# Block 3's x turned by DMA, its second half of attention earlier, and one pair's loads behind an x

## The chip, the cores and the metric

The kernel runs on one core of one Trainium2 chip. The metric is device time in microseconds: the median of several executions. The core has five engines that work side by side, each with its own instruction stream that it runs in order: TensorE (PE in the profile; its weight loads are PEld), VectorE (DVE), ScalarE (ACT), GpSimd (POOL) and SyncE (SP). In this kernel SP issues every DMA. An engine waits for another through semaphores, and everything behind a waiting instruction on its engine waits too.

## The reference, cut to what matters

Sliding-window attention over 8 batches, 8 heads, 576 positions and 64 dimensions, followed by a feed-forward layer with a squared relu:

```
scores = q @ k.T / 8                      # per batch and head
keep only 0 <= i - j < 64                 # causal window of 64 keys
attn   = softmax(scores) @ v
x      = attn, heads side by side         # 4608 tokens x 512
h      = relu(x @ w_in)                   # 512 x 2048
out    = (h * h) @ w_out                  # 2048 x 512
```

Inputs and output are float32; the kernel computes with float16 operands.

## The kernel before, in words

The 4608 tokens are 36 tiles of 128. Two neighbouring tiles are a pair, four tiles (512 tokens) are a block; there are nine blocks, 0 to 8. Pairs 10 and 15 (the names TAILS) hold the last 64 rows of the sequences and have loads of another shape.

For each pair, SP loads k, q and v into staging buffers (L121), POOL casts them to float16 (L269, for tails L761 and L771), and SP turns k and q with DMA transposes into kT and qT (L397). DVE copies the keys that reach over from the pair before (`halo_apart`, L335 to L339). For each tile, TensorE makes the scores (`S_`, L425), ACT the exponentials (`expo`, L431), DVE sets the masked ones to zero (`keep`, L436), TensorE multiplies by v (`V`, L448), and DVE divides by the sums into x_sb (`norm`, L456 and L457). Then x has to be turned, since the next product contracts over its 512 columns. There are two ways in the code: `X` with `copy_xT` turns a tile with four TensorE transposes (L468) into PSUM, and DVE copies it out (L269); `dma_xT` turns a whole pair with one DMA transpose from SP (L477). Either writes into xT, a tile for a block.

Per block, TensorE then makes the first feed-forward product (`UP`, 16 steps of four matmuls, L526). ACT makes the relu of each (L530), and the square is made by ACT (L533) or DVE (L536). The second product (`out_seven`, 14 steps of eight matmuls, L614) is a scheme of seven half-size products in place of eight; DVE makes the sums of operands that it needs (L602) at the start of a block and in between, and sums up and scales the results (L636), which SP stores (L651).

The order is written out by hand. A long list of words (FIRST) gives the order of the start. After it a loop over g from 2 to 9 collects events with due times between 0 and 1, sorts them and records them: the second product of block g − 1, the first product of block g, the attention of block g + 1, and the loads of pairs 2g + 3 and 2g + 4 with the next ones. So every engine's stream, and SP's queue too, follows the due times. `attention(g)` gives the due times of the two halves of a block (a half is a pair): scores at t + 0.02, the product with v at t + 0.25, turning x at t + dx. For block 3 alone, x is turned on TensorE and the times are shifted by 0.1. `loads(p)` gives k and q of pair p + h their transposes at t + 0.06, and asks for the loads of pair a + 1 at t + 0.14 (k and q; for a tail only k) and t + 0.3 (the rest), where a = p + h and t = 0.46 h. For a = 16 the first of them is at t + 0.28.

Buffers that matter here: scores, products with v and transposed x share two PSUM buffers of two banks (`att_bank`, the pool ps_att), taken in turn. The first product's results have two buffers of one bank each (ps_up).

In the profile, block 2's first product begins at 76 us, block 3's at 107 and block 4's at 136. Tiles 12 to 15 are block 3's, so their attention runs beside block 2's products.

Of the kernel before, what the change touches and what calls it, by code (L numbers as in the profile page):

```python
# [40 lines left out]
def kernel(  # L41
# [16 lines left out]
    TAILS = (10, 15)  # L58
# [27 lines left out]
    def later(n, fn):  # L86
        if n == 0:
            fn()
        else:
            put_off.append([n, fn])  # L90

    def tick():
        for e in list(put_off):
            e[0] -= 1
            if e[0] <= 0:
                put_off.remove(e)
                e[1]()
# [65 lines left out]
    def fetch_tail(nm, p):  # L163

        src = {"k": k, "q": q, "v": v}[nm]
        for i in (2 * p, 2 * p + 1):
            if nm == "q":
                if i % 2 == 0:
                    st = two_tiles()
                sts[nm, i] = st[:, i % 2]  # L170
                for n in range(2):
                    fetch_rows(sts[nm, i], src, tail_seq(i) + n, S - 64, 64, 64 * n)
            else:
                st = sts[nm, i] = two_tiles()
                for n in range(2):
                    fetch_rows(st[:, n], src, tail_seq(i) + n, S - 128)
# [88 lines left out]
    def copy(eng, out, in_, scale=1.0):  # L265
        if eng is nc.scalar:
            nc.scalar.activation(out=out, in_=in_, func=AF.Copy, scale=scale)  # L267
        elif scale == 1.0:
            eng.tensor_copy(out=out, in_=in_)  # L269
        else:  # L270
            eng.tensor_scalar(out=out, in0=in_, scalar1=scale, scalar2=None, op0=ALU.mult)
# [19 lines left out]
    def cast_q(i, eng=nc.gpsimd):  # L291
        copy(eng, pair16(q16s, "q16", i // 2)[:, i % 2], sts["q", i])

    def cast_v(i, eng=nc.gpsimd):
        copy(eng, v_evs[i % NV][:, :, 0:D], sts["v", i])
# [15 lines left out]
    def xT_of(g):  # L311
        if g not in xTs:
            xTs[g] = xtp.tile([P, 4, DMC, P], FP16, name="xT", tag="xT")
        return xTs[g]
# [37 lines left out]
    def att_bank(name, dtype=FP32):  # L352
        return ps_att.tile([P, 2, 512], FP32, name=name, tag="ps_a")
# [59 lines left out]
    def S_(i):  # L413
        sc = att_bank("sc")
        scv = sc[:].rearrange("p a (h b t) -> p a h b t", h=HP, b=2)
        for a in range(2 if i < 4 else 0):
            nc.tensor.matmul(sc[:, a, :], ident[:], minus[i > 0], start=True, stop=False,
                             skip_group_check=True)
        for hp in range(HP):
            for blk in range(2):  # L420
                for hh in range(2):
                    r0 = 64 * hh
                    qT = q_cols(i)[r0:r0 + 64, hp, :]
                    qT = qT[:, 64 * blk:64 * blk + 64]
                    nc.tensor.matmul(scv[:, hh, hp, blk, :], keys(i, hp, r0, blk), qT,  # L425
                                     start=i >= 4, stop=True, skip_group_check=i < 4)
        scs[i] = sc
        pms[i] = attw.tile([P, 2, HP * 2 * 64], FP16, name="pm", tag="pm")

    def expo(i, part=slice(0, 2)):  # L430
        nc.scalar.activation(out=pms[i][:, part], in_=scs[i][:, part], func=AF.Exp,  # L431
                             scale=1.0 / float(D) ** 0.5)

    def keep(i, part=slice(0, 2)):
        mask = mask_first if is_first(i) else mask_inner
        nc.vector.tensor_tensor(  # L436
            out=pms[i][:, part], in0=pms[i][:, part],
            in1=mask[:].rearrange("p (o a) r -> p o (a r)", o=1)
            .to_broadcast([P, part.stop - part.start, 512]), op=ALU.min)

    def V(i):
        ps = att_bank("av")
        avs[i] = ps[:, :, 0:4 * 66].rearrange("p a (h e) -> p a h e", h=4)
        for h in range(H):
            for blk in range(2):
                vv = (v_ods if blk == 0 else v_evs)[i % NV]
                h0 = h // 2 * P + blk * 64
                nc.tensor.matmul(  # L448
                    avs[i][64 * blk:64 * blk + 64, h // 4, h % 4, 0:65],
                    pms[i][:, h % 2, h0:h0 + 64], vv[:, h, 0:65], start=True, stop=True)  # L450

    def norm(i):
        if i // 2 not in xs:
            xs[i // 2] = attw.tile([P, 2, 2, HP, D], FP16, name="x_sb", tag="x_sb", bufs=2)
        rden = smallp.tile([P, 2, 4, 1], FP32, name="rden", tag="rden")
        nc.vector.reciprocal(out=rden[:], in_=avs[i][:, :, :, 64:65])  # L456
        nc.vector.tensor_tensor(  # L457
            out=xs[i // 2][:, i % 2], in0=avs[i][:, :, :, 0:D],
            in1=rden[:].to_broadcast([P, 2, 4, D]), op=ALU.mult)

    def xT_cols(i):
        return xT_of(i // 4)[:, i % 4]

    def X(i):
        xps[i] = att_bank("xt_ps")[:, 0, :].bitcast(FP16)[:, 0:DMC * P].rearrange(
            "p (c t) -> p c t", c=DMC)
        for c in range(DMC):
            nc.tensor.transpose(out=xps[i][:, c, :],  # L468
                                in_=xs[i // 2][:, i % 2, c // 2, 2 * (c % 2):2 * (c % 2) + 2, :],
                                identity=ident[:])  # L470

    def copy_xT(i, eng=nc.vector):
        copy(eng, xT_cols(i), xps[i])

    def dma_xT(p):

        nc.sync.dma_start_transpose(  # L477
            out=xT_of(p // 2)[:, p % 2 * 2:p % 2 * 2 + 2].rearrange("p n c t -> p (n c) t"),
            in_=xs[p][:].rearrange("p n a h d -> p (n a h d)"))
# [236 lines left out]
    def attention(g):  # L716
        c = 4 * g
        ev = []
        dx = 0.34 if g == 3 else 0.275

        def sc(i):
            S_(i)
            expo(i)
            later(2, lambda: keep(i))
            tick()

        def to_xT(i):
            if g == 3:
                X(i)
                copy_xT(i)  # L730
                tick()
            else:
                if i % 2:
                    dma_xT(i // 2)

        def va(i):
            V(i)
            norm(i)
            tick()

        for h in range(2):
            a, b, t = c + 2 * h, c + 2 * h + 1, 0.46 * h + (0.1 if g == 3 else 0.0)
            ev += [(t + 0.02, lambda a=a: sc(a)), (t + 0.021, lambda b=b: sc(b)),
                   (t + 0.25, lambda a=a: va(a)), (t + 0.251, lambda b=b: va(b)),
                   (t + dx, lambda a=a: to_xT(a)), (t + dx + 0.0001, lambda b=b: to_xT(b))]
        return ev

    def load(p, part):

        if p in TAILS:  # L750
            for nm in part:
                fetch_tail(nm, p)
        else:
            for nm in part:
                fetch_two(nm, p)
        both = (2 * p, 2 * p + 1)
        if "k" in part:
            for i in both:
                if p in TAILS:
                    k16s["tail", i] = st16.tile([P, 2, H, D], FP16, name="k16", tag="k16")  # L760
                    nc.gpsimd.tensor_copy(out=k16s["tail", i][:], in_=sts["k", i][:])  # L761
                else:
                    cast_k(i)
        if "q" in part:
            for i in both:
                cast_q(i)
        if "v" in part:
            for i in both:
                if p in TAILS:
                    for n, vv in enumerate((v_ods, v_evs)):  # L770
                        nc.gpsimd.tensor_copy(out=vv[i % NV][:, :, 0:D], in_=sts["v", i][:, n])  # L771
                else:
                    cast_v(i)
                    shift_v(i)

    def loads(p):

        ev = []
        for h in range(2):
            t, a = 0.46 * h, p + h  # L780
            if a < NCK // 2:
                ev.append((t + 0.06, lambda a=a: (dma_k(a), dma_q(a))))
                if a not in TAILS:
                    ev.append((t + 0.3, lambda a=a: halo_apart(a)))
            if a + 1 < NCK // 2:
                kq = "k" if a + 1 in TAILS else "kq"
                ev.append((t + (0.28 if a - 1 == TAILS[1] else 0.14), lambda a=a, x=kq: load(a + 1, x)))
                ev.append((t + 0.3, lambda a=a, x=kq: load(a + 1, "kqv"[len(x):])))
        return ev

# [3 lines left out]
    for g in range(2, NTB + 1):  # L794
# [3 lines left out]
        ev = even(out_seven(g - 1))  # L798
# [39 lines left out]
```

## Time and profile before

| | us |
|---|---|
| median of four runs (293.86 to 294.89) | 294.04 |
| profiled execution | 294.03 |
| its span, first to last instruction | 292.0 |
| PE busy | 283.6 (97%) |
| DVE busy | 212.4 (73%) |
| ACT busy | 192.2 (66%) |
| POOL busy | 114.4 (39%) |

A row of the timeline has the start in us from the span's start, the busy time of the row's instructions together, the engine, the line, the operation, what it writes and reads, the shapes and the number of instructions; a bracket tells the idle time before it and what ended it. SPq is SP's queue: the time shown is that of issuing, and the data land some microseconds later. The busy times of matmul rows overlap, since matmuls are pipelined.

### The profile page before, as it was taken

What the parts mean: (1) busy time and instruction counts of PE and PEld (TensorE: products, weight loads), DVE (VectorE), ACT (ScalarE), POOL (GpSimd) and SP (SyncE); (2) the same over time, 40 slices, a digit from 0 to 9 for tenths busy, and PEclk for the clock granted to TensorE, in tenths of its full rate; (3) what the DMA queues carried; (4) which work ended last, traced back from release to release, by engine and by line L of the source; (5) the groups of instructions that cost most, each with busy time, mean ns of one, the idle gap of its engine ahead of it and who ended that gap; (6) DMA issues with size and microseconds to landing.
All of it is one profiled execution on the core that took longest, in us unless ns stands there. A gap on an engine that the chain in (4) does not pass through costs nothing.

```text
span 292.0 us, 7468 instructions
## 1 busy us (share of the span) xinstructions
PE 283.6 (97%) x3039; PEld 195.8 (67%) x3039; DVE 212.4 (73%) x392; ACT 192.2 (66%) x304; POOL 114.4 (39%) x171
## 2 busy tenths in 40 slices
PE   4999999999999999999999999999999999999995
PEld 2678888755666666666666666666666666666684
DVE  3669999867958777776877688768776876555393
ACT  2789898968685666756675767576757675666500
POOL 3703986864348503314555735242455400000000
PEclk9999999999999999999999999999999999999999
DMA  8999999996799168899999999999979801300133
GB/s 217 321 394 318 290 294 323 332 257 147 214 236 238 37 207 192 200 174 263 221 251 196 233 226 187 158 206 231 237 169 259 194 2 50 132 0 2 72 108 110
DMA packets 151842, 57.64 MB, mean 197 GB/s; under 512 B 128256, under 2 KB 143616, under 8 KB 151808
## 3 DMA queue, kind: packets, MB, share of 16 engines
q1 hardware_dynamic: 151808, 57.16, 81.4%
q8 instruction: 24, 0.39, 0.5%
q14 instruction: 10, 0.08, 0.1%
HBM read 38.80 MB, written 9.44 MB: 165 GB/s over the span
## 4 chain that ended last, share of the span: by engine, by line
PE 88%; DVE 5%; DMA 3%; ACT 2%; POOL 0%; issue 0%; SPq 0%
PE hps L526 32%; PE opsC L614 10%; PE opsD L614 8%; PE hps L498 8%; PE opsA L614 8%; PE ops L574 5%; PE opsB L614 4%; PE av L448 4%; PE sc L425 3%; DMA k_st<-in_k_dram 1%; DMA xT<-x_sb 1%; DVE hs_all L602 1%; PE qT_ps L373 1%; DVE pm L436 1%; PE kT_ps L373 1%; PE warm L545 1%
## 5 line engine op out<-in xcount | busy, mean ns | idle before, releaser
L526 PE MATMUL hps<-xT,w_in_sb 128*128 128x512 f16 x448 | 112.9, 379 | 0.4 <-DVE h L536 0.2
L530 ACT ACTIVATE hrelu<-hps 128x512 f32<-128x512 f32 x112 | 66.7, 597 | 64.2 <-PE hps L526 63.9
L614 PEld LDWEIGHTS <-h 128*128 128x128 f16 x624 | 60.4, 98 | 20.7 <-issue 0.2
L526 PEld LDWEIGHTS <-w_in_sb 128*128 128x128 f16 x448 | 42.2, 98 | 33.4 <-DMA xT<-x_sb 0.4
L536 DVE SCALAR_TENSOR_TENSOR h<-hps,hrelu 128x512 f16<-128x512 f32 x54 | 37.2, 689 | 32.8 <-ACT hrelu L530 32.6
L269 POOL COPY v_od<-v_ev 64x512 f16<-64x512 f16 x54 | 37.3, 691 | 10.6 <-ACT v_ev L267 6.8
L431 ACT ACTIVATE pm<-sc 128x1024 f16<-128x1024 f32 (+1 forms) x40 | 35.3, 940 | 4.2 <-PE sc L425 4.2
L533 ACT ACTIVATE h<-hrelu 128x512 f16<-128x512 f32 x58 | 36.5, 629 | 1.6
L614 PE MATMUL opsA<-w_out_sb,h 128*128 128x256 f16 x240 | 31.0, 273 | 0.0
L614 PE MATMUL opsD<-wb_all,h 128*128 128x256 f16 x240 | 31.0, 273 | 0.0
L614 PEld LDWEIGHTS <-hs_all 128*128 128x128 f16 x256 | 25.0, 98 | 8.6
L498 PE MATMUL hps<-xT,w_in_sb 128*128 128x256 f16 x256 | 30.1, 273 | 0.0
L498 PEld LDWEIGHTS <-w_in_sb 128*128 128x128 f16 x256 | 24.2, 98 | 2.9
L457 DVE TENSOR_TENSOR x_sb<-av,rden 128x512 f16<-128x512 f32 x36 | 24.9, 691 | 1.2
L269 POOL CAST k<-kq_st 128x512 f16<-128x512 f32 x17 | 11.6, 686 | 33.8 <-DMA kq_st<-in_k_dram 33.7
L436 DVE TENSOR_TENSOR pm<-pm,mask_inner 128x1024 f16<-128x1024 f16 x25 | 20.1, 807 | 5.7 <-ACT pm L431 5.7
L269 POOL CAST q<-kq_st 128x512 f16<-128x512 f32 x22 | 14.7, 669 | 16.5 <-DMA kq_st<-in_q_dram 16.4
L636 DVE SCALAR_TENSOR_TENSOR osb_all<-opsD,u 128x512 f32<-128x512 f32 x14 | 9.7, 692 | 11.2 <-PE opsD L614 11.0
L614 PE MATMUL opsC<-w_out_sb,h 128*128 128x256 f16 x128 | 16.4, 273 | 0.0
L614 PE MATMUL opsB<-wb_all,hs_all 128*128 128x256 f16 x128 | 16.4, 273 | 0.0
L614 PE MATMUL opsC<-w_out_sb,hs_all 128*128 128x256 f16 x128 | 16.4, 273 | 0.0
L269 POOL CAST v_ev<-kq_st 128x512 f16<-128x512 f32 x16 | 11.6, 728 | 12.2 <-DMA kq_st<-in_v_dram 11.7
(103 smaller groups left out, 372.7 us busy)
## 6 DMA issues: line engine op xcount, KB each, us to landing
kq_st<-in_k_dram SPq DMA_DIRECT2D x26, 256.0 KB, 3.8
kq_st<-in_v_dram SPq DMA_DIRECT2D x24, 256.0 KB, 3.8
out_dram<-osb_all SPq DMA_DIRECT2D x12, 512.0 KB, 4.3
kq_st<-in_q_dram SPq DMA_DIRECT2D x18, 256.0 KB, 4.1
v_st<-in_v_dram SPq DMA_DIRECT2D x16, 256.0 KB, 5.3
k_st<-in_k_dram SPq DMA_DIRECT2D x7, 512.0 KB, 5.9
q_st<-in_q_dram SPq DMA_DIRECT2D x7, 512.0 KB, 5.8
out_dram<-osb_all SPq DMA_DIRECT2D x11, 256.0 KB, 2.4
```

Of the source, the lines that this page charges most:

```text
L269: eng.tensor_copy(out=out, in_=in_)
L431: nc.scalar.activation(out=pms[i][:, part], in_=scs[i][:, part], func=AF.Exp, scale=1.0 / float(D) ** 0.5)
L436: nc.vector.tensor_tensor(out=pms[i][:, part], in0=pms[i][:, part], in1=mask[:].rearrange("p (o a) r -> p o (a r)", o=1) .to_broadcast([P, ...
L448: nc.tensor.matmul(avs[i][64 * blk:64 * blk + 64, h // 4, h % 4, 0:65], pms[i][:, h % 2, h0:h0 + 64], vv[:, h, 0:65], start=True, stop=True)
L457: nc.vector.tensor_tensor(out=xs[i // 2][:, i % 2], in0=avs[i][:, :, :, 0:D], in1=rden[:].to_broadcast([P, 2, 4, D]), op=ALU.mult)
L498: nc.tensor.matmul(hps[:, f, :], w_in_sb[:, c, (2 * j + f) * P:(2 * j + f + 1) * P], xT_of(p // 2)[:, n0:n0 + 2, c, :], start=(c == 0), st ...
L526: nc.tensor.matmul(hps[:], w_in_sb[:, c, f * P:(f + 1) * P], xT_of(g)[:, :, c, :], start=(c == 0), stop=(c == DMC - 1))
L530: nc.scalar.activation(out=hrelu[:], in_=hps[:], func=AF.Relu)
L533: later(2 if f == 0 else 0, lambda: nc.scalar.activation(out=h2_of(g)[:, f, :], in_=hrelu[:], func=AF.Square))
L536: nc.vector.scalar_tensor_tensor(out=h2_of(g)[:, f, :], in0=hps[:], scalar=0.0, in1=hrelu[:], op0=ALU.max, op1=ALU.mult)
L574: nc.tensor.matmul(ops_of[ts][:], h2s[0][:, f, ts * P:(ts + 1) * P], w_out_sb[:, f, :], start=(f == 0), stop=(f == FFC - 1))
L614: nc.tensor.matmul(rows_of(bank, m), a[:, kk, m * P:(m + 1) * P], w[:, kk], start=(first and kk == 0 and (m == 0 or bank in apart)), stop= ...
```

## The change

For block 3, x is turned by `dma_xT` as in the blocks behind it, at t + 0.275. The half that starts at t = 0.56 starts at 0.38; the first stays at 0.1. In `loads`, k and q of pair 11 (a = 10, the first tail pair) are asked for at 0.46 + 0.28 = 0.74 instead of 0.60, which in SP's queue is behind the xT of pair 9, due at 0.735. For a = 16 nothing changes, since TAILS[1] + 1 is 16.

```diff
     def attention(g):
         c = 4 * g
         ev = []
-        dx = 0.34 if g == 3 else 0.275
...
         def to_xT(i):
-            if g == 3:
-                X(i)
-                copy_xT(i)
-                tick()
-            else:
-                if i % 2:
-                    dma_xT(i // 2)
+            if i % 2:
+                dma_xT(i // 2)
...
         for h in range(2):
-            a, b, t = c + 2 * h, c + 2 * h + 1, 0.46 * h + (0.1 if g == 3 else 0.0)
+            a, b = c + 2 * h, c + 2 * h + 1
+            t = (0.1, 0.38)[h] if g == 3 else 0.46 * h
             ev += [(t + 0.02, lambda a=a: sc(a)), (t + 0.021, lambda b=b: sc(b)),
                    (t + 0.25, lambda a=a: va(a)), (t + 0.251, lambda b=b: va(b)),
-                   (t + dx, lambda a=a: to_xT(a)), (t + dx + 0.0001, lambda b=b: to_xT(b))]
+                   (t + 0.275, lambda a=a: to_xT(a)), (t + 0.2751, lambda b=b: to_xT(b))]
...
                 kq = "k" if a + 1 in TAILS else "kq"
-                ev.append((t + (0.28 if a - 1 == TAILS[1] else 0.14), lambda a=a, x=kq: load(a + 1, x)))
+                ev.append((t + (0.28 if a in (TAILS[0], TAILS[1] + 1) else 0.14), lambda a=a, x=kq: load(a + 1, x)))
                 ev.append((t + 0.3, lambda a=a, x=kq: load(a + 1, "kqv"[len(x):])))
```

## The prediction

> **What bounds the kernel now.** I read the busy totals of the page first, then the engine sums over the two stretches that the change touches.
>
> ```profile
> PE 283.6 (97%) x3039; PEld 195.8 (67%) x3039; DVE 212.4 (73%) x392; ACT 192.2 (66%) x304; POOL 114.4 (39%) x171
> 85.00:106.00 21.00, 21.00 (x261) 14.21 (x260) 15.84 (x32) 12.47 (x21) 12.06 (x17) 1.00 0.65 154
> 106.00:136.00 30.00, 29.94 (x318) 19.79 (x312) 21.21 (x37) 20.30 (x33) 8.84 (x12) 1.00 1.00 204
> ```
>
> In the second and third line the columns are the stretch in us, its length, busy time of PE, weight loads, DVE, ACT and POOL, granted clock, DMA share and GB/s. TensorE has work in every microsecond of both (21.00 of 21.00, 29.94 of 30.00) at full clock. So only two things shorten the run: fewer TensorE instructions, or a gap between them that closes. The DMA engines have room in the first stretch (0.65) and none in the second (1.00). The timeline of TensorE then gives the price of each piece by the distance from one start to the next, since the ends are modelled and overlap.
>
> ```profile
> 85.66 1.04 PE L526 MATMUL hps<-xT,w_in_sb 128*128 128x512 f16 x4
> 86.54 1.04 PE L614 MATMUL opsB<-wb_all,hs_all 128*128 128x256 f16 x8
> 87.25 0.69 DVE L457 TENSOR_TENSOR x_sb<-av,rden 128x512 f16<-128x512 f32 x1
> 87.41 1.03 PE L526 MATMUL hps<-xT,w_in_sb 128*128 128x512 f16 x4
> 88.28 0.61 PE L468 MATMUL xt_ps<-ident,x_sb 128*128 128x128 f16 x8
> 88.72 1.04 PE L614 MATMUL opsC<-w_out_sb,hs_all 128*128 128x256 f16 x8
> ```
>
> A group of four L526 or eight L614 matmuls takes 0.87; the eight transposes of two tiles take 88.72 − 88.28 = 0.44.
>
> **Part 1, the transposes leave TensorE.** Tiles 12 to 15 lose X: two groups of eight (88.28, and 102.30 to 102.74), 2 × 0.44 = **−0.88**. All of it is on the path, since TensorE has no idle time there. The four copies xT on DVE (two rows of 0.74 for two) and nothing else go with them; DVE is busy 15.84 of 21.00 and doesn't set the end, so these count zero.
>
> In their place SP issues two DMA transposes, 1.24 us each in an unhurried queue. The row for xT says "DMA to landing us min/median/max: 2.7/3.9/4.7" over ten. The first waits for the second norm of pair 6, at 87.25 + 0.69 = 87.94. SP has issued the v of pair 8 by 84.6 and now stands 3.3 us. Behind it queue, in this order, the k and q of pair 8 (turned at 84.73 and 87.02 before, now about 89.2 and 90.7), four loads of pair 9 (were 88.31 to 91.4, now about 92 to 95), the second xT, two loads of pair 9's v, and the out stores (101.97, which wait for DVE anyway). What is late: k of pair 8 is first read by DVE's halo copy near 98; from 89.2 even the longest kT landing of the trace, 7.4, gives 96.6. Pair 9's v casts end on POOL near 105 instead of 100, and POOL waits from there to 113 for the next load. SP reaches the out stores near 99.5, ahead of their data. So this is hidden, and SP is back in step at 102.
>
> The second xT: V of tiles 14 and 15 now stands at 94.4 to 95.1, the norms take 1.7 us on DVE (86.19 to 87.94 in the pair before), so it is issued near 96.8 and lands near 100.7, 101.5 at the longest. Its reader, the first L526 of block 3, stood at 106.89 and comes to about 106.2. Cover of 4.7 us: zero.
>
> **Part 2, the second half's attention comes sooner.** S of tiles 14 and 15 moves from 92.29 to right behind opsB. This puts a new wait on TensorE. The attention banks are a pool of two: S14 takes the bank of av 12 and S15 that of av 13, which DVE frees at 87.94. TensorE reaches S14 at 87.41 + 0.10 (the gap that every S and V group has ahead of it, as 91.33 to 92.29 is 0.96) = 87.51, and S15 at 87.51 + 0.57/2 = 87.80. It can start 0.05 after DVE's end, 87.99: **+0.19**. Bounds: 0 if the groups lie a little later, 0.6 if DVE's norm is slowed. Behind S15 the whole of TensorE waits, nothing else.
> The two exponentials (1.92 for both) move to 88.0 to 89.9 on ACT. The relu behind them ends at 90.5; the bank it frees is wanted at 91.8. The DVE row of squares that frees the next bank comes to 92.7 against 93.5. Both covered by about 1 us.
>
> **Part 3, pair 11's k and q behind x of pair 9.**
>
> ```profile
> 126.05 1.26 SPq L397 DMA_TRANSPOSE qT<-q  x1
> 127.36 2.07 SPq L121 DMA_DIRECT2D kq_st<-in_k_dram  x2
> 129.48 2.32 SPq L121 DMA_DIRECT2D kq_st<-in_q_dram  x2
> 131.90 2.13 SPq L477 DMA_TRANSPOSE xT<-x_sb  x1
> 136.07 0.55 PEld L526 LDWEIGHTS <-w_in_sb 128*128 128x128 f16 x4 [0.42 <-DMA xT<-x_sb]
> ```
>
> The xT of pair 9 lands at 131.90 + 4.13 = 136.03 and the first L526 of block 4 starts at 136.08. The chain shows this DMA with 1.4% of the span, but the loss is only the gap: opsA in front starts at 134.89 and takes 0.87, so 136.08 − 135.76 = 0.32. Its data (norm of tile 19) are ready at 127.55 + 0.69 = 128.24. After the change it goes out then, shifted with TensorE to near 127.6, and lands by 132.3: **−0.32**, with 3 us to spare.
> What is late next: k and q of pair 11 go out 1.4 us later, and v at about its old time. POOL's casts of q move from 133.78 and 135.03 to about 135.3 and 136.8, v stays near 137.4. This is where DVE makes its sums for block 4 (L436 and L602, from 135.97, now 135.3). The trace has the same meeting two blocks on:
>
> ```profile
> 195.20 1.07 POOL L771 CAST v_od<-kq_st 128x512 f16<-128x512 f32 x1
> 195.82 0.98 DVE L602 TENSOR_TENSOR hs_all<-hs_all,h 128x1024 f16<-128x1024 f16 x1
> 197.74 1.09 DVE L602 TENSOR_TENSOR hs_all<-h 128x1024 f16<-128x1024 f16 x1
> 202.78 1.02 PE L526 MATMUL hps<-xT,w_in_sb 128*128 128x512 f16 x4 [0.17 <-DVE h L536]
> ```
>
> Alone these DVE rows take 0.69 and the cast 0.61. Block 6 has five longer ones, 1.79 us more in all, and TensorE loses 0.34 at 202.78. Block 5 has three (1.09 more) and loses nothing; block 4 now has two. So DVE's slack is about 1.45. The Trainium skill, page "SBUF — State Buffer", section "Who interferes with whom", speaks against the change here: a DVE operation with two SBUF inputs contends with a GpSimd operation that reads SBUF, and the later one blocks until the other has finished. Taken as it stands, up to 0.61 for each of six, 3.7 − 1.45 = 2.2 us of loss; by the rows, 0.40 for each of six at most, 2.4 − 1.45 = 0.95, and for four longer ones 1.6 − 1.45 = 0.15. POOL has a pause near 136 and its copies of 64 partitions slow DVE less than every time (140.05 took 0.69 beside one). I take **+0.10**; bounds 0 and 0.95.
>
> The k of pair 11 lands at 144.22 (7.1 after its issue at 137.09) and DVE's halo copy starts at 144.52. After the change SP gets there at 136.4 to 137.3: its queue runs 0.7 earlier and loses up to 0.9 waiting for the norm. It lands at 143.5 to 144.4, and DVE wants it near 143.5. DVE has 1.09 us of idle time before its next square (146.37), so a wait of up to 0.9 costs zero.
>
> **Sum.** −0.88 + 0.19 − 0.32 + 0.10 = −0.91. The profiled execution took 294.03 (span 292.0 and 2.0 around it), 0.01 from the median of 294.04: 293.12, so **293.1 us**, span 291.1. From block 5 on all queues hang on TensorE's and DVE's data and move along.
>
> **Rivals.**
> - Full gain (both new costs nothing): −1.20, 292.8. For it: the bank and DVE are each within 0.2 us of being ready. Against: 87.94 is DVE's end whatever TensorE does.
> - Most of it given back: DVE and POOL meet in all six rows (0.7 to 0.95) or S15 waits 0.6. Then −0.2 to −0.6, around 293.6. For it: block 6. Against: block 5.
> - No effect: an equal wait takes the place of the transposes, 294.0. It needs an xT that is late by 0.9 at 106.2, so landed at 107.1, 10.3 after issue; the longest is 4.7.
> - **Slower:** k of pair 11 is late. DVE stands in order at the halo copy, the squares behind it hold the hps banks, TensorE stops. It costs nothing until about 144.6, then one for one; to end 0.88 above the median the wait must give 1.8, so a landing after 146.4, 10 us after issue, against 7.4 for the longest of 13. With 146.7 the time is 295.2. For it: the DMA share from 136 to 150 is 1.19, and this landing was among the slowest. Against: the bytes ahead of it are the same.
>
> **Numbers.** 0.3% is 0.88 us, about what a measurement can tell from no change. My forecast 0.52 (own range 292.7 to 293.4; 0.40 of it below 293.16, 0.12 above), full gain 0.10, most given back 0.17, no effect 0.09, slower 0.12. Faster 0.50, same 0.38, slower 0.12. The range that leaves out the slower case and some per cent below is 292.7 to 294.1.
>
> **What would show it.** No L468 after 76 us; block 3's first opsA 0.6 to 0.8 earlier (105.3); a gap of 0.1 to 0.3 in the S matmuls near 87.8, ended by DVE L457; the L526 near 135 without a wait for xT; DVE's L602 of block 4 at 0.98 to 1.09 more often than two times; the halo copy near 143.5 with less than 1 us of idle time ahead. Wrong if S15 waits above 0.6, if an L526 of block 3 waits for xT, if DVE waits for kT near 98 or 143, or if a gap opens later than 150 that wasn't there.

## The result, and the profile after

The changed kernel takes 292.93 us (median of 39 runs, 291.77 to 295.03), against 294.14 for the kernel before on the same chip (60 runs). The ratio is 0.9959 with a 95% interval of 0.9948 to 0.9971: 1.2 us faster, between 0.85 and 1.53. The profiled execution took 292.79 with a span of 291.1 (before: 294.03 and 292.0).

First the page's busy totals of the changed kernel, and the engine sums over the two stretches that the prediction read.

```profile
PE 282.9 (97%) x3023; PEld 194.7 (67%) x3023; DVE 212.6 (73%) x388; ACT 192.6 (66%) x304; POOL 113.5 (39%) x171
85.00:106.00 21.00, 20.93 (x252) 13.95 (x248) 15.36 (x29) 13.47 (x21) 11.14 (x17) 1.00 0.86 185
106.00:136.00 30.00, 30.00 (x313) 19.72 (x311) 21.62 (x38) 20.30 (x32) 9.18 (x13) 1.00 1.07 212
```

PE has 16 matmuls fewer and DVE 4 rows fewer: the transposes and their copies. TensorE is still busy in all but 0.07 us of the 51, at a granted clock of 1.00, so it still sets the end. The DMA share of the first stretch rose from 0.65 to 0.86.

What TensorE loses at a place is worked out below by starts, as in the prediction: the distance from one start to the next, less what the same distance takes elsewhere. The idle time in a bracket is not the same number, since the ends of matmuls are modelled.

Next the timeline around the new place of the second half's scores, weight loads and DVE alone.

```profile
87.05 0.69 DVE L457 TENSOR_TENSOR x_sb<-av,rden 128x512 f16<-128x512 f32 x1
87.31 0.10 PEld L425 LDWEIGHTS <-kh 64*128 64x128 f16 x2 [0.21 <-issue]
87.79 0.29 PEld L425 LDWEIGHTS <-kT 64*128 64x128 f16 x16 [0.19 <-DVE x_sb L457]
88.13 0.55 PEld L526 LDWEIGHTS <-w_in_sb 128*128 128x128 f16 x4
```

The two score tiles take 0.82 from 87.31 to the next group; two tiles elsewhere take 0.57 (in the profile before, 92.29 to 92.86). The wait for DVE's L457, which frees the bank, has therefore cost 0.25.

The last of these views is SP's queue with TensorE at the start of stage 4.

```profile
127.44 1.35 SPq L477 DMA_TRANSPOSE xT<-x_sb  x1
128.84 1.20 SPq L121 DMA_DIRECT2D kq_st<-in_k_dram  x2
130.09 1.64 SPq L121 DMA_DIRECT2D kq_st<-in_q_dram  x2
134.06 1.05 PE L614 MATMUL opsA<-w_out_sb,h 128*128 128x256 f16 x8
134.83 0.64 PEld L526 LDWEIGHTS <-w_in_sb 128*128 128x128 f16 x4
134.94 1.03 PE L526 MATMUL hps<-xT,w_in_sb 128*128 128x512 f16 x4
```

The xT of pair 9 goes out ahead of pair 11's k and q, lands at 131.16 and is read at 134.94 without a wait; the 0.32 that stood here before is gone.

That is not the whole of it. The marks below are the starts of the first opsA row of each pass of the loop; the pass for g is called stage g, and a stage's time holds all its gaps. The prediction calls the start of stage 3 "block 3's first opsA". The expectations go by the block whose second product begins there: their "block 1's first opsA" is the start of stage 2.

| us, one profile each | start of stage 2 | stage 2 | stages 3–4 | stages 5–6 | stages 7–8 | stage 2 to last matmul | median (runs) | ratio, 95% |
|---|---|---|---|---|---|---|---|---|
| before | 75.35 | 30.66 | 58.12 | 58.09 | 54.25 | 213.51 | | |
| changed | 75.38 | 29.80 | 57.80 | 58.07 | 54.59 | 212.66 | 292.93 (39) | 0.9948–0.9971 |
| e1 x by DMA alone | 75.24 | 29.83 | 58.09 | 58.04 | 54.54 | 212.88 | 293.75 (22) | 0.9966–1.0002 |
| e2 load move alone | 74.40 | 30.93 | 57.81 | 57.81 | 54.84 | 213.77 | 294.15 (14) | 0.9976–1.0022 |
| e3 without load move | 74.60 | 29.86 | 57.92 | 57.81 | 54.58 | 212.56 | 293.84 (22) | 0.9976–1.0016 |
| e4 second half at 0.42 | 76.30 | 30.68 | 57.80 | 57.97 | 54.59 | 213.43 | 293.96 (14) | 0.9970–1.0008 |
| e5 second half at 0.46 | 75.77 | 29.61 | 58.11 | 57.89 | 54.25 | 212.24 | 293.13 (22) | 0.9930–0.9965 |
| e6 old times, both others | 74.71 | 29.55 | 57.81 | 57.98 | 54.59 | 212.31 | 292.94 (14) | 0.9938–0.9976 |
| e7 pair 11 still later | 76.25 | 29.92 | 58.48 | 57.93 | 54.59 | 213.30 | 293.84 (18) | 0.9965–1.0001 |
| e8 v loads later | 74.80 | 29.84 | 57.80 | 57.78 | 54.25 | 212.06 | 293.25 (19) | 0.9947–0.9985 |
| e9 0.46, v later | 76.25 | 29.76 | 57.83 | 58.17 | 54.25 | 212.40 | 292.59 (12) | 0.9915–0.9969 |
| e10 old times, v later | 75.61 | 29.74 | 57.80 | 57.90 | 54.25 | 212.08 | 292.58 (10) | 0.9920–0.9970 |
| e11 0.42, masks put off | 74.87 | 30.33 | 57.80 | 57.96 | 54.59 | 213.07 | 292.69 (1) | |
| e12 changed, again | 74.54 | 30.24 | 57.80 | 57.83 | 54.54 | 212.80 | 293.44 (12) | 0.9942–0.9988 |

The median of before beside e1 to e4 was 294.35, beside e5 to e8 294.55, beside e9 to e12 294.19; each ratio is the one on record against runs on the same chip, and is not the quotient of the two medians (for e3 that would be 0.9983). Three things are to be read from this table. The intervals of e1 to e4 and of e7 include 1: by time alone these five are not shown to be faster, and what is said of them below rests on one profile each. The start of stage 2 moves between 74.40 and 76.30, although the work up to there is the same in all of them, so single times carry noise larger than most effects in question; the columns behind it are free of that part. And stages 7–8, which the change doesn't touch, take 54.25 before and 54.59 after.

Where those 0.34 us went shows in the timeline of the changed kernel: DVE's sums with POOL's casts and copies at the start of stage 7, and the first product behind them.

```profile
222.48 0.82 POOL L269 CAST q<-kq_st 128x512 f16<-128x512 f32 x1 [0.34 <-DMA kq_st<-in_q_dram]
222.74 1.10 DVE L602 TENSOR_TENSOR hs_all<-h 128x1024 f16<-128x1024 f16 x1
223.45 0.86 POOL L269 CAST v_ev<-kq_st 128x512 f16<-128x512 f32 x1 [0.15 <-DMA kq_st<-in_v_dram]
223.87 0.98 DVE L602 TENSOR_TENSOR hs_all<-hs_all,h 128x1024 f16<-128x1024 f16 x1
224.38 1.96 POOL L269 COPY v_od<-v_ev 64x512 f16<-64x512 f16 x2
225.79 1.10 DVE L602 TENSOR_TENSOR hs_all<-h 128x1024 f16<-128x1024 f16 x1
226.40 0.95 POOL L269 CAST v_ev<-kq_st 128x512 f16<-128x512 f32 x1
226.92 0.98 DVE L602 TENSOR_TENSOR hs_all<-hs_all,h 128x1024 f16<-128x1024 f16 x1
230.83 0.59 PE L526 MATMUL hps<-xT,w_in_sb 128*128 128x512 f16 x2 [0.18 <-DVE h L536]
```

Five of DVE's six rows at the start of the stage (two masks, L436, and four sums, L602) take 0.98 to 1.10 in place of 0.69 (1.80 us more in all), the squares behind them are late, and TensorE waits for one. Each of the longer rows began while a POOL row ran, and ended 0.54 or 0.55 after that POOL row had ended: 222.48 + 0.82 = 223.30 against 222.74 + 1.10 = 223.84, then 224.31 against 224.85, 226.34 against 226.89, and 227.35 against 227.90. So DVE stood until POOL was done. Before, the six rows were 1.30 longer and nothing waited.

### The profile page after: what moved, and what is told of

It is laid out like the page before. It is cut to its first block, busy times and chain, and to the rows that moved or that the text cites. A ratio compares the mean times of both kernels' runs of the same rounds, so it can differ in the third digit from the quotient of the medians.

```text
span 291.1 us, 7442 instructions
## 1 busy us (share of the span) xinstructions
PE 282.9 (97%) x3023; PEld 194.7 (67%) x3023; DVE 212.6 (73%) x388; ACT 192.6 (66%) x304; POOL 113.5 (39%) x171
## 4 chain that ended last, share of the span: by engine, by line
PE 81%; DVE 8%; DMA 4%; SPq 3%; ACT 3%; issue 1%; ACTq 0%
PE hps L526 29%; PE opsC L614 10%; PE hps L498 9%; PE opsD L614 9%; PE opsA L614 6%; PE ops L574 5%; PE opsB L614 4%; DMA wb_all<-in_moe_w_in_dram 4%; PE av L448 3%; DVE hs_all L602 3%; PE sc L425 3%; DVE x_sb L457 2%; SPq L130 1%; SPq L121 1%; DVE pm L436 1%; ACT pm L431 1%
## 5 line engine op out<-in xcount | busy, mean ns | idle before, releaser
L526 PE MATMUL hps<-xT,w_in_sb 128*128 128x512 f16 x448 | 113.0, 379 | 0.3 <-DVE h L536 0.3
L526 PEld LDWEIGHTS <-w_in_sb 128*128 128x128 f16 x448 | 42.2, 98 | 32.9 <-issue 0.7
L536 DVE SCALAR_TENSOR_TENSOR h<-hps,hrelu 128x512 f16<-128x512 f32 x54 | 37.2, 689 | 32.2 <-ACT hrelu L530 32.0
L269 POOL COPY v_od<-v_ev 64x512 f16<-64x512 f16 x54 | 38.6, 715 | 8.2 <-ACT v_ev L267 4.3
L457 DVE TENSOR_TENSOR x_sb<-av,rden 128x512 f16<-128x512 f32 x36 | 24.9, 691 | 1.2
L436 DVE TENSOR_TENSOR pm<-pm,mask_inner 128x1024 f16<-128x1024 f16 x25 | 19.9, 803 | 3.9 <-ACT pm L431 3.9
L636 DVE SCALAR_TENSOR_TENSOR osb_all<-opsD,u 128x512 f32<-128x512 f32 x14 | 9.7, 692 | 11.6 <-PE opsD L614 11.6
```

The source lines that it names most:

```text
L436: nc.vector.tensor_tensor(out=pms[i][:, part], in0=pms[i][:, part], in1=mask[:].rearrange("p (o a) r -> p o (a r)", o=1) .to_broadcast([P, ...
L457: nc.vector.tensor_tensor(out=xs[i // 2][:, i % 2], in0=avs[i][:, :, :, 0:D], in1=rden[:].to_broadcast([P, 2, 4, D]), op=ALU.mult)
L526: nc.tensor.matmul(hps[:], w_in_sb[:, c, f * P:(f + 1) * P], xT_of(g)[:, :, c, :], start=(c == 0), stop=(c == DMC - 1))
L536: nc.vector.scalar_tensor_tensor(out=h2_of(g)[:, f, :], in0=hps[:], scalar=0.0, in1=hrelu[:], op0=ALU.max, op1=ALU.mult)
L636: nc.vector.scalar_tensor_tensor(out=dst, in0=banks[bank][:, ms], scalar=OUT_SCALE, in1=sums[add][:, ms], op0=ALU.mult, op1=ALU.add)
```

## The experiments

All of them compute the full output.

**Each part alone.** First, x by DMA with the due times and the load as before; second, the load move without the rest; third, the changed kernel without the load move.

```diff
 e1, against the kernel before
-        dx = 0.34 if g == 3 else 0.275
+        dx = 0.275
...
-            if g == 3:
-                X(i)
-                copy_xT(i)
-                tick()
-            else:
-                if i % 2:
-                    dma_xT(i // 2)
+            if i % 2:
+                dma_xT(i // 2)
```

> Block 3's x is turned by DMA, but its second half keeps the old time (t = 0.56) and pair 11 the old loads. My theory: TensorE loses the 32 weight loads and matmuls of the transposes, block 2 is 0.88 shorter, and there is no wait in front of the scores of tile 15. But the norm of tile 15 now ends near 100.9, the xT behind it stands behind an out store in SP's queue, goes out near 101.5 and lands near 104.5 to 106, while the first L526 of block 3 wants it at 106.0: a gap of 0 to 0.5 there. The gap of 0.32 before block 4 stays. Start of block 3's first opsA 0.9 earlier, time 0.4 to 0.9 shorter than before. Rival (the earlier second half is not needed): no gap at block 3's start, a full 0.9. Rival (the earlier second half is all that matters): no gain, the gap at block 3 is 0.9 or more.

Stage 2 took 29.83, of which 0.29 is a gap at its start, so 29.54; before it took 30.66 with a gap of 0.21 there, so 30.45. The transposes' departure is worth 0.91 (predicted 0.88), with no wait for scores. The gap ahead of block 4 stayed:

```profile
101.47 0.38 SPq L651 DMA_DIRECT2D out_dram<-osb_all  x1
101.89 1.59 SPq L477 DMA_TRANSPOSE xT<-x_sb  x1
105.07 1.05 PE L614 MATMUL opsA<-w_out_sb,h 128*128 128x256 f16 x8
105.95 0.59 PE L526 MATMUL hps<-xT,w_in_sb 128*128 128x512 f16 x2
135.10 0.55 PEld L526 LDWEIGHTS <-w_in_sb 128*128 128x128 f16 x4 [0.39 <-DMA xT<-x_sb]
```

The second xT of block 3 lands at 105.49 (3.6 after its issue) and is first read at 105.95. So the old due times leave 0.46 us of cover, as the first rival had it. The last row is pair 9's xT, still late.

```diff
 e2, against the kernel before
-                ev.append((t + (0.28 if a - 1 == TAILS[1] else 0.14), lambda a=a, x=kq: load(a + 1, x)))
+                ev.append((t + (0.28 if a in (TAILS[0], TAILS[1] + 1) else 0.14), lambda a=a, x=kq: load(a + 1, x)))
```

> Only pair 11's k and q are moved behind the xT of pair 9; block 3's x stays on TensorE. My theory: the gap of 0.32 before the first L526 of block 4 closes and nothing else moves: block 4's opsA at the old time, block 5's opsA 0.3 earlier, time 0.3 shorter, unless DVE's sums of block 4 meet POOL's casts in five or six of six rows, when up to 0.35 comes back in block 4. Rival (the xT was covered anyway): no change in any block. Rival (k of pair 11 gets late): a gap in block 4 of 0.5 or more behind DVE's halo copy, time longer by 0.2 or more.

Stages 3–4 took 57.81 (before 58.12): the full 0.31 to 0.32 of part 3. But a gap of 0.55 opened in stage 7, and the time shows no change (294.15; 0.9976 to 1.0022); this interval is too wide to tell 0.3 us from nothing.

```diff
 e3, against the changed kernel
-                ev.append((t + (0.28 if a in (TAILS[0], TAILS[1] + 1) else 0.14), lambda a=a, x=kq: load(a + 1, x)))
+                ev.append((t + (0.28 if a - 1 == TAILS[1] else 0.14), lambda a=a, x=kq: load(a + 1, x)))
```

> The changed kernel with pair 11's loads at the old time. My theory: block 3's opsA 0.6 to 0.8 earlier as in the changed kernel (16 transposes of 0.055 less, the scores of tile 15 wait 0.25), and the gap of 0.3 before block 4's first L526 is back, since the xT of pair 9 still stands behind k and q of pair 11: block 5's opsA 0.3 later than in the changed kernel. Time 0.6 to 0.9 shorter than before. Rival (with TensorE earlier, SP's queue is also earlier and the gap doesn't come back): like the changed kernel, 1.2 shorter.

The score wait is there (0.26). The xT of pair 9 still comes late, but by less than in e1, as this row of the timeline says:

```profile
134.32 0.55 PEld L526 LDWEIGHTS <-w_in_sb 128*128 128x128 f16 x4 [0.22 <-DMA xT<-x_sb]
```

By starts TensorE lost 0.12 there, where 0.3 was expected. Stage 7 has its gap (0.34) without the load move, so that is not its only cause.

**Where the second half's attention stands.** Due at 0.42, behind one more group of the first product, so that the bank would be free; and at 0.46, as in the other blocks.

```diff
 e4, against the changed kernel; e5 has 0.46 in place of 0.42
-            t = (0.1, 0.38)[h] if g == 3 else 0.46 * h
+            t = (0.1, 0.42)[h] if g == 3 else 0.46 * h
```

> The changed kernel with the second half of block 3 at 0.42 in place of 0.38: one group of L526 stands between opsB and the scores of tile 14. My theory: DVE frees the bank of the product with v of tile 13 near 87.7, the scores of tile 15 now come at 88.7, so their wait of 0.25 goes, and the xT of pair 7 (out near 98.5, landed by 102) is still in time for 105.3: block 3's opsA 0.25 earlier than in the changed kernel, time 0.25 shorter than it. Rival (the 0.25 in the scores isn't the wait for the bank): the group of scores still takes 0.82 in place of 0.57.

There was no score wait, but stage 2 lost all the same, 0.88 against the changed kernel: a gap of 1.03 ahead of one L526. DVE's rows in order, and that L526:

```profile
91.53 0.95 DVE L436 TENSOR_TENSOR pm<-pm,mask_inner 128x1024 f16<-128x1024 f16 x1 [0.81 <-ACT pm L431]
92.40 1.09 DVE L602 TENSOR_TENSOR h<-h,hs_all 128x1024 f16<-128x1024 f16 x1
93.42 1.10 DVE L436 TENSOR_TENSOR pm<-pm,mask_inner 128x1024 f16<-128x1024 f16 x1
94.44 0.68 DVE L536 SCALAR_TENSOR_TENSOR h<-hps,hrelu 128x512 f16<-128x512 f32 x1
95.17 1.02 PE L526 MATMUL hps<-xT,w_in_sb 128*128 128x512 f16 x4 [0.86 <-DVE h L536]
```

The masks (L436) stand ahead of the square (L536) in DVE's order. DVE waited 0.81 for the exponential, its three rows, each begun while POOL ran, were 1.07 longer than 0.69, and the square that frees a bank ended at 95.12. Both were needed: 1.07 sooner the square would have ended at 94.05, ahead of 94.15, when its L526 was due.

> The changed kernel with block 3's second half at 0.46, the step between the halves that all later blocks have. My theory: opsC stands between V and the scores, so the bank of tile 13 is free and the wait of 0.25 goes; the masking of tile 14 comes behind the DVE square that frees the next hps bank, so the gap of 1.03 of the run at 0.42 doesn't come; the xT of pair 7 lands near 102, wanted at 105. From block 1's to block 3's first opsA 29.8 less any wait at the first (before 30.66, changed 29.80), block 3's to block 5's as in the changed kernel (57.8). Rival (DVE's order is as bad as at 0.42): a gap of 0.5 to 1 at 93 to 96.

At 0.46 there is neither a score wait nor this gap, and stage 2 takes 29.61. The loss in this profile lies elsewhere: in stage 4 five of DVE's six rows were long, 1.81 us in all, and TensorE lost 0.32.

```profile
135.33 1.12 DVE L436 TENSOR_TENSOR pm<-pm,mask_inner 128x1024 f16<-128x1024 f16 x1 [0.22 <-ACT pm L431]
136.37 1.09 DVE L602 TENSOR_TENSOR hs_all<-h 128x1024 f16<-128x1024 f16 x1
```

The masks' place in e4 was then tested: those of tiles 14 and 15 were put off by two more steps.

```diff
 e11, against e4
-            later(2, lambda: keep(i))
+            later(4 if i in (14, 15) else 2, lambda: keep(i))
```

> The run at 0.42 with the masking of tiles 14 and 15 put off by two more steps, so that it stands behind the DVE square that frees an hps bank, not ahead of it. My theory (DVE stood at the masking waiting for the exponential, and the square behind it freed the bank too late): the gap of 1.03 near 94 goes; V of tile 15 may now wait up to 0.5 for its mask. Rival (the gap comes from ACT's two exponentials, which hold up the relu): a gap of 0.8 or more stays before that L526.

The gap of 1.03 is gone, since the square now goes ahead of both masks. The product with v of tile 15 waits instead:

```profile
91.45 0.69 DVE L536 SCALAR_TENSOR_TENSOR h<-hps,hrelu 128x512 f16<-128x512 f32 x1 [1.35 <-ACT hrelu L530]
93.86 0.68 DVE L436 TENSOR_TENSOR pm<-pm,mask_inner 128x1024 f16<-128x1024 f16 x1
94.60 0.33 PEld L448 LDWEIGHTS <-pm 128*64 128x64 f16 x16 [0.63 <-DVE pm L436]
```

That costs 0.72, so stage 2 takes 30.33. Without the masks ahead of it the square is in time, so their place is one of the two conditions of e4's gap, and the rival (ACT's exponentials holding up the relu) is out. The other condition isn't tested by e11, whose DVE rows from 87.6 to 94.5 took 0.68 or 0.69 each, so that POOL held none of them; that it was needed is only worked out above. Putting the masks off moves most of the loss to another place.

**Is the earlier second half needed?** The changed kernel with the old due times (scores at 0.56), both other parts kept.

```diff
 e6, against the changed kernel
+        dx = 0.275
...
-            a, b = c + 2 * h, c + 2 * h + 1
-            t = (0.1, 0.38)[h] if g == 3 else 0.46 * h
+            a, b, t = c + 2 * h, c + 2 * h + 1, 0.46 * h + (0.1 if g == 3 else 0.0)
```

> Block 3's x by DMA with the old times of attention (second half at 0.56), and pair 11's loads behind the xT of pair 9: the changed kernel without its second edit. My theory: no wait in the scores (0.25 less than the changed kernel), no gap before block 3 (the xT landed 0.46 ahead of its use in the run with the old times; this cover is thin, so 0 to 0.3), none before block 4 (0.3 less than the run with the old times alone). Block 1's to block 3's first opsA 29.5 plus the wait at the first, block 3's to block 5's 57.8. Rival (the earlier second half is what makes block 4's gap close): a gap of 0.3 before block 4.

Stage 2 is 0.25 shorter than in the changed kernel, exactly the score wait, and no gap stands ahead of blocks 3 or 4. The xT of pair 7 goes out late but is in time: it lands at 104.66, 0.48 before its reader.

```profile
101.08 1.60 SPq L477 DMA_TRANSPOSE xT<-x_sb  x1
105.14 1.03 PE L526 MATMUL hps<-xT,w_in_sb 128*128 128x512 f16 x4
```

So part 2 gave cover that wasn't wanted (in the changed kernel this xT landed at 100.22, 5.8 ahead of its reader at 106.06) and cost 0.25. The medians, 292.94 and 292.93, don't separate the two.

**Pair 11 later still**, to find where late keys begin to cost: the slower rival.

```diff
 e7, against the changed kernel
-                ev.append((t + (0.28 if a in (TAILS[0], TAILS[1] + 1) else 0.14), lambda a=a, x=kq: load(a + 1, x)))
+                ev.append((t + (0.52 if a == TAILS[0] else 0.28 if a == TAILS[1] + 1 else 0.14), lambda a=a, x=kq: load(a + 1, x)))
```

> The changed kernel with pair 11's k and q asked for at 0.98 in place of 0.74, behind its v and both out stores: this measures the cover of the last step. My theory: k lands in its turned form near 145 to 146 in place of 141.5, DVE stands at the halo copy for about 2 (it was there at 143.3), 1.1 of it is DVE's idle time, so TensorE gets a gap of 0.5 to 1.2 in block 4. Rival (the halo copy has more cover than that, since TensorE needs it only for the scores of tile 22 at 146.5): DVE waits and TensorE has no gap. Rival (a late k costs more than one for one, since q comes behind it): a gap of 2 or more.

```profile
136.12 1.07 DVE L436 TENSOR_TENSOR pm<-pm,mask_inner 128x1024 f16<-128x1024 f16 x1 [0.22 <-ACT pm L431]
137.11 1.09 DVE L602 TENSOR_TENSOR hs_all<-h 128x1024 f16<-128x1024 f16 x1
144.47 0.68 DVE L536 SCALAR_TENSOR_TENSOR h<-hps,hrelu 128x512 f16<-128x512 f32 x1
145.20 1.02 PE L526 MATMUL hps<-xT,w_in_sb 128*128 128x512 f16 x4 [0.38 <-DVE h L536]
145.34 0.23 DVE L339 COPY kh<-kT 128x256 f16<-128x256 f16 x1
```

It didn't answer its question. The keys landed at 145.32, 3.8 later than in the changed kernel, yet the halo copy waited less than 0.2 for them, because DVE itself was late: its six rows were 2.16 longer and TensorE lost 0.69 by waiting for squares ahead of the copy. At what landing the keys begin to cost is open. What e7 shows in its place is the prediction's other rival, DVE and POOL meeting in all six rows: 0.69, near its 0.7 to 0.95.

**The new gap in stage 7.** The v loads of second halves asked for later, so that POOL's v work meets fewer of DVE's sums; then the same with the second half at 0.46, and with the old times.

```diff
 e8, against the changed kernel; e9 is e5 with this line, e10 is e6 with it
-                ev.append((t + 0.3, lambda a=a, x=kq: load(a + 1, "kqv"[len(x):])))
+                ev.append((t + (0.42 if h and a + 1 not in TAILS else 0.3), lambda a=a, x=kq: load(a + 1, "kqv"[len(x):])))
```

> The changed kernel with the v loads of each loop's second pair at 0.88 in place of 0.76 (tails as they were), so that POOL casts v about 3.5 later and DVE makes its sums at a block's start alone. My theory (the gaps of 0.3 in blocks 6 and 7 come from DVE rows that are stretched beside POOL): in block 7 the sums take 0.68 each but for one or two beside the q casts, the gap near 229.6 goes; in block 6, where the tail's casts stay, the gap near 200.4 stays. Time 0.3 shorter than the changed kernel. Rival (the gaps come from DVE's own load): no change in block 7.

```profile
221.91 1.09 DVE L602 TENSOR_TENSOR hs_all<-h 128x1024 f16<-128x1024 f16 x1
223.04 0.69 DVE L602 TENSOR_TENSOR hs_all<-hs_all,h 128x1024 f16<-128x1024 f16 x1
226.28 0.69 DVE L536 SCALAR_TENSOR_TENSOR h<-hps,hrelu 128x512 f16<-128x512 f32 x1 [0.32 <-ACT hrelu L530]
229.66 1.03 PE L526 MATMUL hps<-xT,w_in_sb 128*128 128x512 f16 x4
```

The gap is gone: stages 7–8 take 54.25 again, and the L526 at 229.66 stands without a wait. Stages 5–6 went from 58.07 to 57.78 too, although the gap in stage 6 was expected to stay; why it went is not settled. The time that was to follow, 0.3 less than the changed kernel, is not shown: the median is 293.25. The timelines say when POOL's first v cast begins, counted from the start of stage 7, what the six DVE rows took beyond 0.69 each, and what TensorE lost:

| stage 7, us | before | e5 | e12 | changed | e2 | e8 | e10 |
|---|---|---|---|---|---|---|---|
| v cast begins | 2.69 | 2.79 | 2.54 | 2.40 | 1.88 | 4.18 | 4.11 |
| DVE rows longer by | 1.30 | 1.38 | 1.75 | 1.80 | 2.04 | 0.69 | 0.49 |
| TensorE lost | 0 | 0 | 0.30 | 0.35 | 0.55 | 0 | 0 |

> The second half at 0.46 and the later v loads together. My theory: no wait in the scores of tile 15 (0.25 less than the changed kernel), no gap in block 7 (0.35 less). From block 1's to block 3's first opsA 29.55 to 29.65, block 5's to block 7's and on to block 9's 57.8 and 54.25; block 3's to block 5's 57.8, with up to 0.3 more where POOL's casts of pair 11 meet DVE's sums in five or six rows. From block 1's first opsA to the end 215.1 to 214.5, against 215.7 in the changed kernel. Rival (the v casts only move the meeting to another place): a gap of 0.3 at another block's start.

No gap in stage 7 and none in stage 4; stage 5 has one of 0.37 instead, with rows 1.82 longer, as the rival had it (e8 and e10, with the same line, have none there), and the start of stage 2 one of 0.21. Median 292.59.

> Old times of attention in block 3, x by DMA, pair 11's loads behind an x, and the later v loads. My theory: as the run at 0.46, but v of pair 9 and an out store change places in SP's queue ahead of the xT of pair 7, whose cover was 0.5 to 1: a gap of 0 to 0.3 before block 3. From block 1's first opsA to the end 215.1 to 214.5. Rival (the thin cover breaks): a gap of 0.5 or more at block 3's first L526, block 1's to block 3's first opsA unchanged but block 3's to block 5's 58.3 or more.

From stage 3 on, TensorE loses no more than 0.08 at any place; stage 2 has the 0.19 at its start alone. From stage 2 to the last matmul this is 0.58 less than the changed kernel. Its profiled execution took 1.5 to 1.7 longer than the others behind the last matmul (4.71 against 3.0 to 3.2); I have no reason for that. Median 292.58.

**The changed kernel once more**, beside e9 and e10 on their chip.

> The changed kernel once more. My theory: the wait of 0.2 to 0.3 in the scores of tile 15 comes again, since it is written in the order; the gap of 0.3 at the start of block 6 or 7 may be there or not, since it hangs on how POOL's casts and DVE's sums fall; the first opsA of block 1 lies anywhere from 74.4 to 76.3, as in the runs so far. Rival (the trace is the same each time): all three as in the first profile.

The median was 293.44. The gap in stage 7 is there again (0.30), and the score wait is 0.48 this time: the halo copy of keys (L338) took 0.46 in place of 0.24, standing until a POOL cast was done, so that the norm that frees the bank ended later against TensorE.

```profile
84.46 0.46 DVE L338 COPY kh<-kT 128x256 f16<-128x256 f16 x1
87.39 0.29 PEld L425 LDWEIGHTS <-kT 64*128 64x128 f16 x16 [0.42 <-DVE x_sb L457]
```

The intervals of e9, e10 and e12 overlap, so by time neither is shown to be faster than the changed kernel; by the traces from stage 2 on, e8 (212.06) and e10 (212.08) are the shortest.

## Why the prediction was right

It held: 293.1 was forecast, 292.93 measured, and the sum of −0.91 stands against −0.85 from stage 2 to the last matmul, −0.95 for the span, and −1.2 (0.85 to 1.53) for the medians. The parts that were priced came out well; that the whole agrees so closely is in part luck. In this pair of profiles the change made −0.90 + 0.25 − 0.32 in stages 2 to 4, −0.02 in stages 5–6 and +0.34 in stages 7–8, together −0.65. The other 0.20 of the 0.85 is the gap at the start of stage 2 that the profile of before happened to have:

```profile
76.43 0.55 PEld L526 LDWEIGHTS <-w_in_sb 128*128 128x128 f16 x4 [0.32 <-DVE xT L269]
```

The medians fell by more than 0.65. Without stages 7–8 the parts make −0.99, which is inside their interval; the interval of the repeat, e12, is 0.35 to 1.71 and holds both. That would fit if the kernel before often has the gap of stage 7 too, but it has one profile alone, and this stays open. By its steps:

- **Transposes off TensorE, −0.88.** −0.91 by e1 and −0.90 by e6, with the gaps at the stage's start taken off. The price by distance between starts was right, and nothing on SP's queue came late: the keys of pair 8 landed at 91.86 and were first read at 99.14.
- **The score bank, +0.19.** 0.25 here, 0.26 in e3 and e8, 0.37 in e7, 0.48 in e12. The mechanism and the releaser were right, and so was the distance: DVE's norm ended 0.43 after the first score matmul's start, as in the working (87.31 and 87.74 here, 87.51 and 87.94 there). What was too small came from halving the 0.57: S15's first matmul doesn't stand 0.285 behind S14's, but 0.24 (92.53 for 92.29 in the profile before). Anything that delays that norm counts in full: 0.54 after the first matmul in e7, 0.65 in e12.
- **"Both covered by about 1 us", of the exponentials and the square behind them.** For the square this step was wrong, without a cost: it ended at 93.19, 0.17 ahead of its L526.

```profile
88.25 1.10 DVE L602 TENSOR_TENSOR h<-h 128x1024 f16<-128x1024 f16 x1
91.49 1.09 DVE L602 TENSOR_TENSOR h<-h,hs_all 128x1024 f16<-128x1024 f16 x1
92.51 0.68 DVE L536 SCALAR_TENSOR_TENSOR h<-hps,hrelu 128x512 f16<-128x512 f32 x1
93.36 0.59 PE L526 MATMUL hps<-xT,w_in_sb 128*128 128x512 f16 x2
```

DVE had no idle time from 87.66 on, and no mask waited for ACT. But these two rows and the second mask took 1.09 or 1.10 in place of 0.68, 1.24 more together, because POOL ran when they began; in the profile before, one row of this stretch was longer (1.04). The working moved DVE's rows and left out that more of them then meet POOL. In e4, where the masks also waited for ACT, the same step cost 1.03.
- **The gap ahead of block 4, −0.32.** −0.32 here (58.12 to 57.80), and the same in e2 alone.
- **DVE and POOL in block 4, +0.10.** Nothing: the six rows were 1.21 longer, and the slack was worked out as 1.45. In e5 they were 1.81 longer and 0.32 was lost, within the bounds of 0 to 0.95. The trace agrees with the Trainium skill's rule, page "SBUF — State Buffer", section "Who interferes with whom": the one that comes later waits until the other has finished. From 75 us on, the 14 profiles have 1232 such DVE rows (L436 and L602). Of 368 that took over 0.72, every one began while a POOL instruction ran and ended 0.54 or 0.55 after its end. Of 811 that began while none ran, not one took more. The other 53 began with at most 0.17 of a POOL instruction left, or within 0.02 of its start, and were not held. What was too high is the price that the working took from the rule, 0.61 for each row. A held row ends 0.54 after POOL's end and not 0.69, and a cast that was itself held behind a DVE row has at most 0.55 left when the next row begins, which makes 0.55 + 0.54 − 0.69 = 0.40. So the estimate "by the rows" was the rule's own price. And the row at 140.05, beside a copy and not longer, isn't a weaker effect of copies: it began before the copy did (140.09), and POOL waited.
- **"From block 5 on all queues hang on TensorE's and DVE's data and move along."** This step failed, and with it one of the prediction's own signs of being wrong came true: a gap later than 150 that wasn't there. POOL's casts hang on DMA landings, which don't move along with TensorE, and their phase against DVE's sums changed: +0.35 in stage 7. In the span it was offset by the gap of 0.21 at the start of stage 2, and by 0.12 less behind the last matmul. That gap comes and goes between profiles (e1, e2, e9, e10 and e12 have 0.18 to 0.49) and is no gain of the change.
- **Halo copy of pair 11.** Keys landed at 141.53 and the copy began at 143.38, without a wait; predicted were 143.5 to 144.4. The slower rival never came near; where its price begins stays open, since e7 missed it.

The stage 7 loss is tied to how long DVE's six rows are. In the 14 profiles, stages 4 to 7 give 56 such starts. Leaving out the three where xT itself was late (before, e1 and e3 in stage 4), TensorE lost at most 0.08 in each of the 33 with up to 1.53 of excess, and in the 20 above lost the excess less 1.45, within 0.04: 0.12 at 1.57, 0.22 at 1.67, 0.35 at 1.80, 0.55 at 2.04, 0.69 at 2.16. The slack of 1.45 that the prediction took from block 6 alone holds in all of them. That the phase of the v cast decides the excess in stage 7 is shown by e8, e9 and e10, which moved it. That the change brought the gap is less sure: of the 11 profiles with the v loads at their old place, nine have it, e2 with block 3's x still on TensorE among them, and only those of before and e5 have not. Why the casts come earlier in the changed kernel than before, and not in e5, is not settled: there is one profile of before and one of e5, and DMA landings differ between executions (pair 11's keys took 5.97 from issue to landing in the changed kernel and 6.39 in e12).

## What to carry to other kernels

When an edit gives an engine more slack, measure the cover that was there first: here the two larger parts alone did the work, and the earlier second half brought the cover to 5.8 us where 0.46 was enough, for a wait of 0.25. Work out cover along the order of the engine that delivers, with every instruction ahead of the wanted one and what that one waits for. Where two engines hold each other up, count which row of one begins while the other runs, price each from a trace, and set the sum against the slack in every stage behind the edit, not only in the one edited.

## What the hardware showed

DVE and POOL held each other up one instruction at a time; they did not share. A DVE operation on two SBUF operands of 128x1024 float16 took 0.68 or 0.69 alone. If it began while POOL ran a cast or copy with more than 0.17 to go, it ended 0.54 or 0.55 after POOL's end, which made 0.98 to 1.13 in most cases and 1.45 in the longest, behind a cast of 1.04. The other way round, 422 of the 454 POOL casts and copies that began within such a row ended 0.47 or 0.48 after it. The halo copies of keys (L338 and L339, 0.16 to 0.23 alone) that took over 0.25 all ended 0.08 after a POOL instruction, one of them after 1.09. DVE's operations with an operand in PSUM (L457, L536, L636) were not held: 518 of them began while POOL ran, and took 0.67 to 0.69.

In this kernel the loss on TensorE has a sharp threshold: 1.45 us of longer rows among the six at a stage's start is free, and the rest is paid one for one. And one kernel's runs spread over 3.3 us (291.77 to 295.03). In the 14 profiles the start of stage 2 differs by 1.9 us though the instructions up to there are the same; in the two of the changed kernel it differs by 0.84 (75.38 and 74.54), and the time from there to the last matmul by 0.14.
